# Log-sum rows of the dense units: four small products of a block-diagonal tile, copied to the queries by ScalarE or VectorE in turn

## The chip, the core and the metric

The kernel runs on one core of a Trainium2 chip. The time is that of the device for one execution, in microseconds (us); the median of three runs is compared. The engines, by the profile's names: PE (TensorE, the matmuls; PEld is its loading of weights), DVE (VectorE), ACT (ScalarE), POOL (GpSimd) and SP (SyncE, which issues DMAs here). They run side by side, each in the order of its own instructions, and wait for each other through semaphores. A matmul writes to PSUM; ScalarE and VectorE read it from there.

## The reference

Two attention layers over 2048 positions of 1024 features, with 32 heads of 32 each, and their outputs side by side. Layer B is a sliding window of 256 keys, layer A a dilated window of 8 keys.

```python
def _B_ref(x, wqkv, wo):
    B, S, D = x.shape
    H = 32; Dh = D // H; W = 256
    qkv = (lambda x, *d: x.transpose(*d))((x @ wqkv).reshape(B, S, 3, H, Dh), 2, 0, 3, 1, 4)
    q, k, v = qkv[0], qkv[1], qkv[2]
    scores = jnp.einsum("bhqd,bhkd->bhqk", q, k) * (Dh ** -0.5)
    idx = jnp.arange(S)
    mask = (idx[:, None] - idx[None, :] >= 0) & (idx[:, None] - idx[None, :] < W)
    scores = jnp.where(mask[None, None], scores, -1e9)
    p = _softmax(scores, axis=-1)
    o = jnp.einsum("bhqk,bhkd->bhqd", p, v)
    return (lambda x, *d: x.transpose(*d))(o, 0, 2, 1, 3).reshape(B, S, D) @ wo
```

`_A_ref` has the same projections; each query sees the 8 keys at distances 0, 2, ... 14.

## The kernel before

The work is cut into 8 units of 512 rows: four of layer B (dense) and then four of layer A (windowed). A unit has 8 groups of 4 heads, so there are 32 dense groups. All projections (q and k at L518, v at L583, the output at L645) split each operand into a high and a low part and add three products; the splits are made by `Stream.parts` (L201, L204, L207) from weights that POOL's queue loads (L159).

A dense group is done in two passes. The first (`first`, L857) computes the scores of 128 queries by up to 384 keys, takes the row maximum on VectorE (L862, into `nm`) and the exponential with its row sum on ScalarE (L867, into `sm`): 16 blocks, one for each of 4 query blocks b and 4 heads j. When all 16 are through, `log_sum` takes the logarithm of the sums (L880) and forms `nl` = -(maximum + log-sum), 128 queries by 16, with a high and a low part in `hl` (L885 to L888). `rows` brings these 32 columns into 32 rows of a PSUM tile by one product with the identity (L896), and `spread` writes them to the lower 32 partitions of the stacked queries `q[96:P, j, :]`, once for each head, times a 0/1 tile `pick` which keeps of each row only the block and head that it belongs to (L902). The keys hold ones in these partitions. So the second pass (`second`, L940), which computes the scores again with keys as rows, subtracts maximum and log-sum in the product itself, and its exponential (L947) is the finished probability. Masks are applied by POOL (L926) or VectorE (L929), and `values` multiplies with v (L987).

PSUM is held by rings: 3 tiles for projections, 4 for the scores of both passes and the log-sum rows, 1 for the output of a group.

The order of all instructions is made when the kernel is built. `Clock` books the assumed time of every instruction on its engine. The loop at L1060 takes, from four lists (the log-sum products, the second pass, the first pass, the projections), the item that can start first; an item names its due time by what it waits for, for the second pass `h["rows"]` of its heads and a free PSUM tile (L970). Work of the other engines is issued when the clock reaches it. Waits themselves are put in from what each instruction reads and writes, and hold whether or not the clock foresaw them.

`constants` builds the identity, the masks and `pick` on POOL at the start, ahead of the first loads that POOL issues.

Of the kernel before, what the change touches and what calls it, by code (L numbers as in the profile page):

```python
# [7 lines left out]
F32 = mybir.dt.float32  # L8
# [6 lines left out]
P = 128  # L15
# [21 lines left out]
CW = 1.36  # L37
ORDER = (0, 1, 2, 3, 4, 5, 6, 7)
BANK_LATE = 0.0
EARLY, WARM = 1.0, 10  # L40
TERMS = ((0, 0), (0, 1), (1, 0))

# [174 lines left out]
def kernel(ctx, tc, xs, wqk, wv, wo, outs, units):  # L217
# [87 lines left out]
    def constants():  # L305
        def bands(name, n, keep, fill, *conds):
            m = const.tile([P, n], F32, name=name) if isinstance(name, str) else name
            nc.gpsimd.memset(m, keep)
            for step, base, chan in conds:
                nc.gpsimd.affine_select(m, m, pattern=[[step, n]], compare_op=ALU.is_ge, fill=fill, base=base,  # L310
                                        channel_multiplier=chan)
            return m

        ident = cst["ident"] = const.tile([P, P], F32R, name="ident")
        keep = const.tile([P, P], F32, name="keep_d")
        nc.gpsimd.memset(keep, 0.0)
        nc.gpsimd.affine_select(ident, keep, pattern=[[-1, P]], compare_op=ALU.not_equal, fill=1.0, base=0,
                                channel_multiplier=1)
        pick = cst["pick"] = pickp.tile([32, 16], F32, name="pick")
        nc.gpsimd.memset(pick, 0.0)  # L320
        for row in (0, 16):
            nc.gpsimd.affine_select(pick, pick, pattern=[[-1, 16]], compare_op=ALU.not_equal, fill=1.0, base=-row,
                                    channel_multiplier=1)
        cst["mask_d"] = bands("mask_d", 384, 0.0, FAR, (1, -1, -1), (-1, 256, 1))
        near = cst["near"] = band0[:, :200].rearrange("p (v c) -> p v c", v=5)
        nc.gpsimd.memset(near, 0.0)
        for i in range(4):
            part = near[32 * i:32 * i + 32]
            for step, base, chan in ((1, -1, -1), (-1, 8, 1)):
                nc.gpsimd.affine_select(part, part, pattern=[[0, 5], [step, 40]], compare_op=ALU.is_ge, fill=FAR,  # L330
                                        base=base, channel_multiplier=chan)
        nc.gpsimd.affine_select(near[0:32, 0, :], near[0:32, 0, :], pattern=[[1, 40]], compare_op=ALU.is_ge, fill=FAR,
                                base=-8, channel_multiplier=0)
        cst["keep_f"] = bands("keep_f", P, BIG, 0.0, (-1, -1, 1))
        cst["keep_d"] = bands(keep, P, BIG, 0.0, (1, 0, -1))
        ck.use("pool", 3.0, ck.now)

        def ones():
            zero = cst["mask_d"][96:P, None, P:2 * P].to_broadcast([32, 24, P])
            for t in kst:  # L340
                nc.scalar.activation(t[96:P, :, :].rearrange("p j (a s) -> p (j a) s", s=P), zero, AF.Identity,
                                     bias=1.0, scale=1.0)
                ck.use("act", 2.7, ck.now)

        ck.defer(24.0, ones)

    pfree = [0.0]
    vbuf = [const.tile([P, 6, n * P], F32, name=f"vbuf{i}") for i, (_, n) in enumerate(VPARTS)]
    vpart = {s0 + i: (p, i * P) for p, (s0, n) in enumerate(VPARTS) for i in range(n)}
    tails = const.tile([P, NG, 8], F32, name="tails")  # L350
# [41 lines left out]
    def latest(*ts):  # L392
        return None if any(t is None for t in ts) else max(ts)
# [440 lines left out]
    def attention(u, s):  # L834
# [43 lines left out]
        def log_sum():  # L878
# [4 lines left out]
            def parts():  # L883
                nl = small.tile([P, 16], F32, tag="nl", name="nl")
                nc.vector.tensor_tensor(nl, h["nm"], ln, op=ALU.subtract)  # L885
                hl = small.tile([P, 2, 16], F32R, tag="hl", name="hl")
                nc.vector.tensor_copy(hl[:, 0, :], nl)
                nc.vector.tensor_tensor(hl[:, 1, :], nl, hl[:, 0, :].bitcast(F32), op=ALU.subtract)  # L888
                e2 = ck.use("dve", 0.52, e, port=True)
                aux.append(Item(lambda: latest(rs.when(BANK_LATE), e2), lambda: rows(hl), 0.08))  # L890

            ck.defer(e, parts)

        def rows(hl):
            ps, bank = rs.take()
            nc.tensor.matmul(ps[0:32, 0:P], hl.rearrange("p a b -> p (a b)"), cst["ident"], start=True, stop=True)  # L896

            def spread():

                h["rows"] = []  # L900
                for j in range(4):
                    nc.vector.tensor_tensor(q[96:P, j, :].rearrange("p (b s) -> p b s", s=P),  # L902
                                            ps[0:32, None, 0:P].to_broadcast([32, 4, P]),
                                            cst["pick"][0:32, 4 * j:4 * j + 4, None].to_broadcast([32, 4, P]), op=ALU.mult)
                    e = ck.use("dve", 0.61, ck.now)
                    h["rows"].append(e + ROWS_LATE)
                rs.give(bank, e)

            return spread

# [220 lines left out]
```

## Time and profile before

| What | us |
|---|---|
| runs, median (lowest to highest) | 1831.32 (1831.26 to 1832.84) |
| the profiled execution: its span | 1830.6 |
| TensorE busy | 1807.8 |
| VectorE busy | 1202.9 |
| ScalarE busy | 889.4 |
| POOL busy | 394.4 |

The profiled execution is one of its own; its span is the time from its first to its last instruction. A row of the groups names the line, the engine, the operation, what is written and read with shapes, and the count; behind the bar stand the busy time of all of them, the mean duration of one in ns, and the engine's idle time before them with what ended it. A row of the timeline begins with the start and the duration in us. A row of the waits gives who waited for whom: us in total, how often, the longest. Busy time of TensorE counts each matmul from its start to its modelled end, and these overlap; what one costs is the distance between starts.

### The profile page before, as it was taken

To read this page: it belongs to the slowest core of one execution; us is meant where nothing else is said; L and a number is where in the kernel's file an instruction comes from. 1 tells how busy PE (TensorE), PEld (TensorE's weight loads), DVE (VectorE), ACT (ScalarE), POOL (GpSimd) and SP (SyncE) were. 2 spreads that over 40 slices of the span, in tenths; PEclk is the share of its full clock that TensorE was granted. 3 is DMA by queue.
4 is the path that set the end of the run, shared out by engine and by line. 5 is a ranking of instruction groups with operands and counts; after the bars stand their busy time and mean duration, and the time that the engine had idled before them with its cause. 6 is when DMAs were issued, how large, how long until landed. Compare 5 with 4: busy or idle time off the path is not lost.

```text
span 1830.6 us, 38331 instructions
## 1 busy us (share of the span) xinstructions
PE 1807.8 (99%) x14826; PEld 1477.5 (81%) x14826; DVE 1202.9 (66%) x2694; ACT 889.4 (49%) x2254; POOL 394.4 (22%) x926
## 2 busy tenths in 40 slices
PE   9999999999999999999999999999999999999998
PEld 7787777888778888788887788888888788888887
DVE  6677886768867669777777564655547445655463
ACT  5556466565655655656555343433425234423331
POOL 3322323233242324332233200110001000100000
PEclk9999999999999999999999999999999999999999
DMA  8455665545656456455554343444334443534432
GB/s 242 121 138 139 176 164 150 170 121 160 164 155 164 136 151 183 125 157 141 141 142 130 110 135 116 152 143 130 119 115 143 133 138 108 162 107 128 127 104 83
DMA packets 109141, 257.43 MB, mean 141 GB/s; under 512 B 14496, under 2 KB 29856, under 8 KB 108960
## 3 DMA queue, kind: packets, MB, share of 16 engines
q0 software_dynamic: 41760, 152.06, 28.1%
q1 hardware_dynamic: 56832, 83.00, 17.6%
q10 hardware_dynamic: 10368, 19.93, 3.0%
q8 instruction: 117, 1.92, 0.5%
q14 instruction: 64, 0.52, 0.1%
HBM read 164.63 MB, written 23.07 MB: 103 GB/s over the span
## 4 chain that ended last, share of the span: by engine, by line
PE 92%; DVE 4%; DMA 2%; ACT 2%; issue 1%; SPq 0%; ACTq 0%; POOL 0%; DVEq 0%; POOLq 0%
PE g L518 37%; PE g L645 19%; PE g L583 17%; PE s L940 5%; PE s L857 5%; PE o L987 5%; PE s L711 2%; PE o L774 2%; DMA raw<-xs 1%; DVE w L207 1%; DVE s L862 1%; ACT s L867 0%; DMA qst<-nat 0%; DMA pbuf<-nat 0%; DVE x L207 0%
## 5 line engine op out<-in xcount | busy, mean ns | idle before, releaser
L518 PE MATMUL g<-x,w 128*128 128x512 f32 x3072 | 770.2, 394 | 3.8 <-DVE nm L729 2.4
L518 PEld LDWEIGHTS g<-x,w 128*128 128x128 f32 x3072 | 566.3, 189 | 114.2 <-issue 8.3
L583 PE MATMUL g<-w,x 128*128 128x256 f32 (+1 forms) x2304 | 391.9, 320 | 0.9 <-issue 0.7
L207 DVE TENSOR_TENSOR w<-raw,w 128x512 fp32r<-128x512 f32 x516 | 338.6, 698 | 52.0 <-ACT w L201 44.8
L583 PEld LDWEIGHTS g<-w,x 128*128 128x128 f32 x2304 | 332.3, 190 | 29.2 <-DVE w L207 1.8
L645 PE MATMUL g<-ot,w 128*128 128x512 f32 x1416 | 343.6, 393 | 3.7 <-DVE ot L826 1.8
L867 ACT ACTIVATE s<-s,nm 128x384 f32<-128x384 f32 (+2 forms) x512 | 274.3, 536 | 102.1 <-DVE nm L862 101.8
L862 DVE CUSTOM_DVE_ANT_0 s<-s,mask_d 128x384 f32<-128x384 f32 (+2 forms) x512 | 261.5, 553 | 88.2 <-PE s L857 87.5
L645 PEld LDWEIGHTS g<-ot,w 128*128 128x128 f32 x1416 | 262.4, 188 | 59.3 <-DVE ot L826 3.2
L926 POOL TENSOR_SCALAR_AFFINE_SELECT pbuf<-pbuf 128x128 f32<-128x128 f32 (+1 forms) x606 | 219.8, 391 | 325.1 <-ACT pbuf L947 323.8
L947 ACT ACTIVATE pbuf<-s 128x384 f32<-128x384 f32 (+2 forms) x480 | 202.7, 505 | 72.2 <-PE s L940 70.2
L159 POOL DMA_DIRECT2D raw<-wqk x126 | 68.1, 540 | 457.5 <-DVE w L207 356.3
L204 DVE CAST w<-raw 128x1024 fp32r<-128x1024 f32 x205 | 141.7, 691 | 24.8 <-PE g L518 24.0
L940 PEld LDWEIGHTS s<-qst,kst 128*128 128x128 f32 x704 | 113.0, 188 | 41.2 <-ACT s L867 16.3
L857 PE MATMUL s<-kst,qst 96*128 96x384 f32 (+2 forms) x512 | 142.4, 342 | 0.9 <-ACT s L867 0.6
L940 PE MATMUL s<-qst,kst 128*128 128x256 f32 (+2 forms) x704 | 136.5, 302 | 3.5 <-ACT s L867 3.0
L719 DVE TENSOR_TENSOR band<-s,near 128x160 f32<-128x160 f32 x128 | 32.4, 315 | 158.0 <-PE s L711 158.0
L536 ACT COPY ost<-g 128x512 f32<-128x512 f32 x54 | 31.7, 587 | 207.1 <-PE g L645 200.4
L857 PEld LDWEIGHTS s<-kst,qst 96*128 96x128 f32 x512 | 93.4, 189 | 26.2 <-issue 4.7
L826 DVE TENSOR_TENSOR ot<-o,ot 128x512 fp32r<-128x512 f32 x64 | 44.0, 688 | 101.6 <-ACT ot L822 101.4
L867 ACT ACTIVATION_READ_ACCUMULATOR s<-s,nm 128x1 f32 x512 | 105.3, 206 | 0.0
L159 POOL DMA_DIRECT2D raw<-wo x64 | 34.2, 534 | 304.2 <-DVE w L207 260.2
(77 smaller groups left out, 1298.6 us busy)
## 6 DMA issues: line engine op xcount, KB each, us to landing
raw<-wqk POOLq DMA_DIRECT2D x126, 512.0 KB, 4.3
raw<-wv POOLq DMA_DIRECT2D x72, 512.0 KB, 5.1
raw<-wo POOLq DMA_DIRECT2D x64, 512.0 KB, 4.1
qst<-nat SPq DMA_DIRECT2D x96, 256.0 KB, 5.3
kst<-nat SPq DMA_DIRECT2D x96, 256.0 KB, 5.6
raw<-xs POOLq DMA_DIRECT2D x28, 512.0 KB, 4.6
outs<-ost ACTq DMA_DIRECT2D x56, 256.0 KB, 2.3
kst<-halo SPq DMA_DIRECT2D x72, 128.0 KB, 4.5
```

Source lines behind the costliest of these rows:

```text
L159: (self.nc.scalar if early else self.nc.gpsimd).dma_start(raw if len(ap.shape) == 2 else raw.rearrange("p (a b) -> p a b", a=2), ap)
L204: nc.vector.tensor_copy(t[:, 0, :], raw)
L207: nc.vector.tensor_tensor(t[:, 1, c:c + 512], raw[:, c:c + 512], t[:, 0, c:c + 512].bitcast(F32), op=ALU.subtract)
L518: nc.tensor.matmul(h["ps"], h["w"][:, a, k * P:(k + 1) * P], xt[u][k][:, b, :], start=(k == 0 and i == 0), stop=(k == NK - 1 and i == 2))
L583: nc.tensor.matmul(ps, xt[u][kw * g + k][:, a, p0:p0 + P], h["w"][g][:, c, k], start=(first and t == 0 and half == 0), stop=(last and t == 2),
L645: nc.tensor.matmul(h["ps"], w[:, a, c:c + P], ot[u, k][:, b, :], start=(k == 0 and i == 0), stop=(k == NK - 1 and i == 2))
L857: nc.tensor.matmul(ps[:, :n], q[0:96, j, b * P:(b + 1) * P], kk[0:96, j, c0:c1], start=True, stop=True)
L862: nc.vector.tensor_tensor_reduce(ps[:, :n], ps[:, :n], mask[:, cut:full], scale=-1.0, scalar=BIG, op0=ALU.add, op1=ALU.min, accum_out=nm)
L867: nc.scalar.activation(ps[:, :n], ps[:, :n], AF.Exp, bias=nm, scale=-1.0, accum_out=sm)
L926: nc.gpsimd.affine_select(w, w, pattern=[[0, m], [step, n]], compare_op=ALU.is_ge, fill=0.0, base=base, channel_multiplier=chan)
L940: nc.tensor.matmul(ps[:, i * n:(i + 1) * n], kk[:, j, 256 + kb * P:256 + (kb + 1) * P], q[:, j, q0:q0 + n], start=True, stop=True)
L947: nc.scalar.activation(w, ps[:, :pack * n].rearrange("p (j n) -> p j n", j=pack), AF.Exp)
```

## The change

The 32 columns of `hl` are laid into a tile `turn` of 132 columns, in four blocks of 32 whose starts are 32 apart: block b holds only the values of query block b, at columns 4j + b (high) and 16 + 4j + b (low), and zeros elsewhere. `turn` is cleared once at the start; each group writes the same places again. Four products with the identity, one for each b, fill 32 rows by 512 columns of one PSUM tile. `pick` shrinks to 4 columns: a row is kept for head j or not. Each of the four copies to `q[96:P, j, :]` is then a product with one number per row, and may be done by ScalarE or VectorE; the planner takes the engine that its clock says ends first (0.62 for ScalarE, 0.61 for VectorE), and books them side by side. The booked cost of the products goes from 0.08 to 0.3. `pick` is built by 32 selects of one column in place of 2 of 16.

```diff
-        pick = cst["pick"] = pickp.tile([32, 16], F32, name="pick")
+        pick = cst["pick"] = pickp.tile([32, 4], F32, name="pick")
         nc.gpsimd.memset(pick, 0.0)
-        for row in (0, 16):
-            nc.gpsimd.affine_select(pick, pick, pattern=[[-1, 16]], compare_op=ALU.not_equal, fill=1.0, base=-row,
-                                    channel_multiplier=1)
+        for row in range(0, 32, 4):
+            for b in range(4):
+                c = row // 4 % 4
+                nc.gpsimd.affine_select(pick[:, c:c + 1], pick[:, c:c + 1], pattern=[[0, 1]], compare_op=ALU.not_equal,
+                                        fill=1.0, base=-row - b, channel_multiplier=1)
+        nc.gpsimd.memset(turn, 0.0)
...
+    turn = const.tile([P, 132], F32, name="turn")
...
-                hl = small.tile([P, 2, 16], F32R, tag="hl", name="hl")
-                nc.vector.tensor_copy(hl[:, 0, :], nl)
-                nc.vector.tensor_tensor(hl[:, 1, :], nl, hl[:, 0, :].bitcast(F32), op=ALU.subtract)
+                hl = turn[:, :132].rearrange("p (b x) -> p b x", x=33)
+                hi, lo = [hl[:, :, 16 * a:16 * a + 16:4].bitcast(F32R) for a in range(2)]
+                by = nl.rearrange("p (j b) -> p b j", b=4)
+                nc.vector.tensor_copy(hi, by)
+                nc.vector.tensor_tensor(lo, by, hi.bitcast(F32), op=ALU.subtract)
                 e2 = ck.use("dve", 0.52, e, port=True)
-                aux.append(Item(lambda: latest(rs.when(BANK_LATE), e2), lambda: rows(hl), 0.08))
+                aux.append(Item(lambda: latest(rs.when(BANK_LATE), e2), rows, 0.3))
...
-        def rows(hl):
+        def rows():
             ps, bank = rs.take()
-            nc.tensor.matmul(ps[0:32, 0:P], hl.rearrange("p a b -> p (a b)"), cst["ident"], start=True, stop=True)
+            for b in range(4):
+                nc.tensor.matmul(ps[0:32, b * P:b * P + P], turn[:, 32 * b:32 * b + 32].bitcast(F32R), cst["ident"],
+                                 start=True, stop=True)
...
                 for j in range(4):
-                    nc.vector.tensor_tensor(q[96:P, j, :].rearrange("p (b s) -> p b s", s=P),
-                                            ps[0:32, None, 0:P].to_broadcast([32, 4, P]),
-                                            cst["pick"][0:32, 4 * j:4 * j + 4, None].to_broadcast([32, 4, P]), op=ALU.mult)
-                    e = ck.use("dve", 0.61, ck.now)
-                    h["rows"].append(e + ROWS_LATE)
-                rs.give(bank, e)
+                    if ck.ends("act", 0.62, ck.now) <= ck.ends("dve", 0.61, ck.now) + SPREAD:
+                        nc.scalar.activation(q[96:P, j, :], ps[0:32, :], AF.Copy, scale=cst["pick"][:, j:j + 1])
+                        ends.append(ck.use("act", 0.62, ck.now))
+                    else:
+                        nc.vector.tensor_scalar(q[96:P, j, :], ps[0:32, :], cst["pick"][:, j:j + 1], None, op0=ALU.mult)
+                        ends.append(ck.use("dve", 0.61, ck.now))
+                    h["rows"].append(max(ends) + ROWS_LATE)
+                rs.give(bank, max(ends))
```

`SPREAD` is 0. Since the planner orders everything anew, other instructions move too. In the built program the counts change like this:

| Engine | Before | After |
|---|---|---|
| TensorE, products for the log-sum rows | 32 | 128 |
| VectorE, copies to the queries | 128 | 62 |
| ScalarE, copies to the queries | 0 | 66 |
| VectorE / ScalarE, evacuations of v (L539 / L536) | 10 / 54 | 17 / 47 |
| VectorE / POOL, mask instructions (L929 / L926) | 130 / 606 | 132 / 604 |
| POOL, selects for `pick` | 2 | 32 |

The order around one dense group of the changed program (the 13th, as an example), with the engines that an instruction waits for:

```
TensorE  small product of turn, ident      [VectorE, ScalarE]   x4
TensorE  v projection, 256 columns                              x18
TensorE  second pass, heads 0 to 3         [VectorE, ScalarE] [ScalarE] [VectorE] [ScalarE]
VectorE  copy to the queries, head 0       [TensorE]
ScalarE  copy to the queries, head 1       [VectorE]
VectorE  copy to the queries, head 2       [ScalarE]
ScalarE  copy to the queries, head 3       [VectorE]
```

More of the change, by code (lines that the diff above doesn't have):

```diff
@@ L39 @@
 BANK_LATE = 0.0
+SPREAD = 0.0
 EARLY, WARM = 1.0, 10
@@ L898, in spread @@
             def spread():
                 h["rows"] = []
+                ends = []
                 for j in range(4):
-                    nc.vector.tensor_tensor(q[96:P, j, :].rearrange("p (b s) -> p b s", s=P),
-                                            ps[0:32, None, 0:P].to_broadcast([32, 4, P]),
-                                            cst["pick"][0:32, 4 * j:4 * j + 4, None].to_broadcast([32, 4, P]), op=ALU.mult)
-                    e = ck.use("dve", 0.61, ck.now)
-                    h["rows"].append(e + ROWS_LATE)
```

## The prediction

> **What bounds the kernel now.** I read the page first: busy shares, the strips of 40 slices, the chain of waits.
>
> ```profile
> PE 1807.8 (99%) x14826; PEld 1477.5 (81%) x14826; DVE 1202.9 (66%) x2694; ACT 889.4 (49%) x2254; POOL 394.4 (22%) x926
> ...
> PE   9999999999999999999999999999999999999998
> ...
> DVE  6677886768867669777777564655547445655463
> ACT  5556466565655655656555343433425234423331
> ...
> PE 92%; DVE 4%; DMA 2%; ACT 2%; issue 1%; SPq 0%; ACTq 0%; POOL 0%; DVEq 0%; POOLq 0%
> ```
>
> TensorE is busy in every slice and holds 92% of the chain. VectorE has slack even in the dense units (the first 22 slices, digits 5 to 8). So another matmul costs its full time, and VectorE time saved is worth only what TensorE waits for today. Next I asked for busy time by stretch, and for the waits of TensorE and of its weight loads, in the dense units alone (31 to 1020 us):
>
> ```profile
> 31.00:1020.00 989.00, 980.30 (x5959) 792.38 (x5958) 744.47 (x1927) 576.97 (x1681) 299.60 (x741) 1.00 0.55 150
> ...
> PE s L896 <- DVE hl L888: 3.6, 4, 2.0
> PE s L940 <- ACT s L867: 3.0, 4, 1.1
> ...
> PEld s L940 <- ACT s L867: 16.3, 27, 1.6
> ...
> PEld s L857 <- ACT s L867: 3.7, 15, 0.9
> ```
>
> TensorE (the first busy figure) idles 989.0 - 980.3 = 8.7 us there, 3.6 us of it at L896 for VectorE's log-sum parts. No row of these waits names the copies of L902: all of them are hidden. The third view, groups by line, holds the replaced copies and their nearest relatives (after the bar: busy us, mean ns of one, then idle time before them):
>
> ```profile
> L902 DVE TENSOR_TENSOR qst<-s,pick 32x512 fp32r<-32x512 f32 x128 | 79.3, 676 | 9.9 <-PE s L896 9.4
> ...
> L459 DVE SCALAR_TENSOR_TENSOR nat<-g,nat 128x512 fp32r<-128x512 f32 x64 | 44.0, 688 | 43.5 <-ACT nat L455 43.4
> L455 ACT ACTIVATE nat<-g 128x512 fp32r<-128x512 f32 x64 | 38.3, 598 | 95.2 <-PE g L518 88.6 <-DMA qst<-nat 6.1 <-ACT s L867 0.5
> L536 ACT COPY ost<-g 128x512 f32<-128x512 f32 x54 | 31.7, 587 | 207.1 <-PE g L645 200.4 <-PE s L940 5.5 <-DMA kst<-nat 1.2
> L947 ACT ACTIVATE pbuf<-s 128x384 f32<-128x384 f32 (+2 forms) x480 | 202.7, 505 | 72.2 <-PE s L940 70.2 <-POOL pbuf L926 0.6
> ```
>
> **The change part by part. First the matmuls.** One product of 128 columns becomes four in each of the 32 dense groups: 96 more. Two places of the timeline show the price:
>
> ```profile
> 395.00 0.22 PE L896 MATMUL s<-ident,hl 128*32 128x128 f32 x1
> ...
> 395.06 0.74 PE L857 MATMUL s<-kst,qst 96*128 96x384 f32 x3
> 395.26 2.48 DVE L902 TENSOR_TENSOR qst<-s,pick 32x512 fp32r<-32x512 f32 x4 [0.22 <-PE s L896]
> ...
> 178.15 0.18 DVE L888 TENSOR_TENSOR hl<-nl,hl 128x16 fp32r<-128x16 f32 x1
> ...
> 178.47 0.22 PE L896 MATMUL s<-ident,hl 128*32 128x128 f32 x1 [1.99 <-DVE hl L888]
> ...
> 178.53 1.65 PE L583 MATMUL g<-w,x 128*128 128x256 f32 x12
> ...
> 180.01 0.34 PE L940 MATMUL s<-qst,kst 128*128 128x384 f32 x1
> ```
>
> The next product starts 0.06 us after L896 both times, so the row's 0.22 us is mostly pipeline. 96 x 0.06 = 5.8 us, all on the path. If each had instead to wait out its own 32-column weight load (0.11 us in the row below) it were 10.6 us; below 0.06 I see no reason to go.
>
> ```profile
> 394.89 0.11 PEld L896 LDWEIGHTS s<-ident,hl 128*32 128x32 f32 x1
> ```
>
> **The copies.** Four VectorE copies per group become 66 on ScalarE and 62 on VectorE over the kernel. VectorE's new form (one PSUM operand, a scale per partition) has no row; it lies between L902 at 0.676 and L459 at 0.688 us, so 0.68. ScalarE's is nearest L455, 0.60; L536's 0.587 is the other end. If each engine ran its two alone, the rows would be complete after two copies. The built program says otherwise: in the usual group VectorE's first copy waits for TensorE, ScalarE's first for VectorE's first, VectorE's second for ScalarE's first, ScalarE's second for VectorE's second. All four read one PSUM tile, and the chain is strict. The planner books the two engines side by side (0.62 and 0.61) and places the score products L940 for that. So the stall to price is TensorE arriving before the fourth copy. The price of a hand-over, from two pairs of rows:
>
> ```profile
> 36.88 0.14 DVE L862 DVE_READ_ACCUMULATOR2_ANT nm<- 128x1 f32 x1
> ...
> 37.06 0.45 ACT L867 ACTIVATE s<-s,nm 128x256 f32<-128x256 f32 x1 [1.64 <-DVE nm L862]
> ...
> 19.09 0.60 ACT L455 ACTIVATE nat<-g 128x512 fp32r<-128x512 f32 x1 [4.93 <-PE g L518]
> ...
> 19.72 0.69 DVE L459 SCALAR_TENSOR_TENSOR nat<-g,nat 128x512 fp32r<-128x512 f32 x1 [4.46 <-ACT nat L455]
> ```
>
> VectorE to ScalarE 37.06 - 37.02 = 0.04, back 0.03; VectorE to TensorE 178.47 - 178.33 = 0.14. Counted from the start of the last small product: first copy from 0.26 (395.26 - 395.00) to 0.94; second 0.98 to 1.58; third 1.61 to 2.29; fourth 2.33 to 2.93; TensorE may go at 3.07. Before, the fourth ended at 0.26 + 2.48 = 2.74, on one engine. The hand-overs eat the whole gain.
>
> When does TensorE come? In 12 of the 32 groups the built program has nine 512-column products (or eighteen of 256) behind the small ones, then L940 for heads 0 to 3 in a row. A 256-column product takes (180.01 - 178.53) / 12 = 0.123; a 512-column one 10.88 / 48 = 0.227:
>
> ```profile
> 1101.60 10.88 PE g L645 x48
> ```
>
> Head 3 is then due at 0.06 + 9 x 0.227 + 3 x 0.06 = 2.28 (nine groups) or 2.45 (three), and stalls 0.79 or 0.62 us: 9 x 0.79 + 3 x 0.62 = 9.0 us. In these groups nothing stands on VectorE between the parts and the first copy, so it does start at 0.26. Nine more groups come by the same sum to 0.45 twice and 0.44 (head 3 due at 2.6), 0.1 three times (due at 2.96), about 1 twice (a weight split stands before VectorE's copies) and 1.6 once (head 0 due at 0.3): together 5.2 us. The other 11 have enough products in between. Stalls: 14.2 us. Both ends: 0, if TensorE comes later than the built order says; 14.2 + 21 x 0.4 = 22.6 us if each of the four hand-overs takes 0.1 more.
>
> **What queues behind the waiting copies.** ScalarE is held from its first wait to 2.93. In eight groups an evacuation of 512 columns (0.59) stands next, and only then the first exponential of L940's results, which must free a PSUM bank: 2.93 + 0.59 + 0.45 (256 columns, as at 37.06 above) = 3.97. TensorE, having gone on at 3.07 with four 256-column products, wants the bank at 3.6: 0.35 x 8 = 2.8 us, between 0 and double. VectorE is free at 2.29 instead of 2.74; what waits there, mainly weight splits, gains nothing that TensorE waits for.
>
> [...]
>
> **The start.** 32 selects of one column replace two of 16, ahead of the first weight loads on POOL:
>
> ```profile
> 1.49 0.45 POOL L322 TENSOR_SCALAR_AFFINE_SELECT pick<-pick 32x16 f32<-32x16 f32 x2
> ...
> 10.02 1.19 POOL L159 DMA_DIRECT2D raw<-wqk  x2 [0.30 <-issue]
> ...
> 20.32 0.68 DVE L204 CAST w<-raw 128x1024 fp32r<-128x1024 f32 x1
> ...
> 22.43 5.44 ACT L341 ACTIVATE kst<-mask_d 32x3072 fp32r<-32x3072 f32 x2
> ...
> raw<-wqk POOLq DMA_DIRECT2D x126, 512.0 KB, 4.3
> ```
>
> 30 x 0.2 plus a memset of 0.2 move the load from 10.0 to 16.2; landing after 4.3 it is there at 20.5, where the cast now starts at 20.32: 0.2 us, and between 0 and 2. The masks behind the selects come 6 us later too, all issued by 16 us; the first reader in this view, L341, starts at 22.43. The four-column pick and the strided parts (16 elements each, like L888's) I cost at nothing.
>
> **Sum.** 5.8 + 14.2 + 2.8 + 0.2 = 23.0 us on the profiled span of 1830.6; the median of the runs is 0.7 above it. Forecast 1854.3, rounded to 1854, 1.2% slower. Its own range takes half to one and a half of the two waits (17.0 us) and the matmuls at 5.8 to 10.6: 1845 to 1867.
>
> **Rivals.** A: the copies' chain is hidden, because TensorE itself runs behind the planner's clock, as the copies of L902 were. Then 5.8 to 6.6 us: 1838. For it: today nothing waits for L902. Against: today L940 comes where the planner put it for four serial copies.
> B, the other side: VectorE's relief. 66 x 0.68 = 45 us less work in the dense units lets the row maxima come earlier, the exponentials too, and so the PSUM banks that L940 and L857 wait for. Price: at most those weight-load waits, 16.3 + 3.7 = 20.0 us, and what is left of the 8.7 us of idle. It decides from 5.8 us on, if the chain of copies costs nothing; half of the 20 gives 5.8 - 10 = -4.2: 1827. Against it: 744 of 989 us busy, and a VectorE held at each ScalarE copy.
> C: ScalarE's holding spreads: in every group the later PSUM banks come two exponentials of L947 late, 2 x 0.505 us; 32 x 1.0 + 14.2 + 5.8 = 52 us: 1883. Against: ScalarE is 58% busy there (577 of 989) and catches up in a few us.
>
> **How the numbers follow.** Forecast 0.72, A 0.13, B 0.08, C 0.07. The range 1838 to 1868 adds A to the forecast's own and leaves out B and C. A measurement of this kernel can tell 0.2% (3.7 us) from no change. Faster: most of B, 0.06; within: the rest of B and A's edge, 0.06; slower 0.88.
>
> **What would show it.** Small products 0.06 us apart and 128 of them; copies alternating on the two engines without overlap, the fourth ending near 2.9; TensorE waiting before L940 for ScalarE's copies, some 14 us in all, where L902 had none; the first weight load issued near 16 us. Copies that overlap, or no such waits, would make me wrong.

## The result and the profile after

| | before | changed |
|---|---|---|
| median of the runs, us | 1831.29 (4 runs) | 1882.97 (1880.78 to 1885.20, 4 runs) |
| ratio | 1 | 1.0282, 95% interval 1.0267 to 1.0296 |
| span of the profiled execution, us | 1830.6 | 1880.8 |

The change costs 51.6 us, 29 more than the forecast and 15 above the end of its range. (Where effects are given in us below, they are differences of ratios times 1831.3, since each group of runs had its own runs of the kernel before. A range in brackets behind an effect goes by the intervals of the ratios.) The page of the changed kernel, in the lines that answer to those of before: busy times, and the chain of waits by engine and by line.

```profile
PE 1846.0 (98%) x14922; PEld 1494.8 (79%) x14922; DVE 1168.5 (62%) x2633; ACT 935.1 (50%) x2317; POOL 409.5 (22%) x955
...
PE 88%; DVE 4%; ACT 3%; DMA 2%; issue 1%; POOL 1%; POOLq 0%; ACTq 0%; DVEq 0%; SPq 0%
PE g L523 36%; PE g L650 18%; PE g L588 16%; PE s L952 5%; PE s L862 4%; PE o L999 4%; PE s L716 2%; PE o L779 2%; DVE qst L916 2%; DMA raw<-xs 1%; ACT qst L913 1%; DVE x L208 1%; DVE w L208 1%; DVE s L867 1%; ACT s L872 0%
```

The lines of the chain before:

```profile
PE g L518 37%; PE g L645 19%; PE g L583 17%; PE s L940 5%; PE s L857 5%; PE o L987 5%; PE s L711 2%; PE o L774 2%; DMA raw<-xs 1%; DVE w L207 1%; DVE s L862 1%; ACT s L867 0%; DMA qst<-nat 0%; DMA pbuf<-nat 0%; DVE x L207 0%
```

Two things meet the eye. The copies (L916 on VectorE, L913 on ScalarE) stand in the chain with 2% and 1%, 51 us of steps, where L902 is not listed. And TensorE is busy 38 us longer although 96 short products are all that was added to it: a matmul that takes longer is busy, too, so something has slowed matmuls that did not change. The stretch of the dense units (31 us to shortly before the first windowed unit), the waits of TensorE and VectorE, and the copies among the groups by line. A row of a stretch gives its bounds and length, then the busy time and count of TensorE, its weight loads, VectorE, ScalarE and POOL, and last the granted clock, the DMA share and GB/s:

```profile
31.00:1072.00 1041.00, 1019.87 (x6122) 813.43 (x6121) 712.00 (x1869) 623.83 (x1751) 312.29 (x753) 0.99 0.51 144
```

```profile
PE s L952 <- ACT qst L913: 7.1, 19, 0.8
PE s L862 <- ACT s L872: 5.1, 6, 1.2
PE s L952 <- DVE qst L916: 3.8, 7, 1.5
...
DVE x L205 <- DMA raw<-xs: 21.3, 4, 6.9
```

```profile
L916 DVE TENSOR_SCALAR qst<-s,pick 32x512 fp32r<-32x512 f32 x62 | 45.8, 743 | 43.1 <-ACT qst L913 25.0 <-PE s L904 17.9
L913 ACT ACTIVATE qst<-s,pick 32x512 fp32r<-32x512 f32 x66 | 43.6, 675 | 91.0 <-DVE qst L916 81.2 <-PE s L904 9.5
```

TensorE now waits 7.1 + 3.8 = 10.9 us for the copies before the second pass, and 5.1 us for exponentials of the first pass. Each engine waits for the other's copy: 25.0 us on VectorE, 81.2 us on ScalarE. The copies take 0.743 and 0.675 us where 0.61 and 0.62 are booked. One group in the timeline, TensorE's rows, then VectorE's, then ScalarE's:

```profile
407.89 0.40 PE L904 MATMUL s<-ident,turn 128*32 128x128 f32 x4
408.13 2.36 PE L588 MATMUL g<-w,x 128*128 128x256 f32 x18
410.32 0.61 PE L952 MATMUL s<-qst,kst 128*128 128x128 f32 x3
411.32 1.03 PE L952 MATMUL s<-qst,kst 128*128 128x128 f32 x6 [0.38 <-ACT qst L913]
...
408.33 0.74 DVE L916 TENSOR_SCALAR qst<-s,pick 32x512 fp32r<-32x512 f32 x1 [0.99 <-PE s L904]
409.82 0.74 DVE L916 TENSOR_SCALAR qst<-s,pick 32x512 fp32r<-32x512 f32 x1 [0.74 <-ACT qst L913]
...
409.11 0.68 ACT L913 ACTIVATE qst<-s,pick 32x512 fp32r<-32x512 f32 x1 [2.55 <-DVE qst L916]
410.59 0.68 ACT L913 ACTIVATE qst<-s,pick 32x512 fp32r<-32x512 f32 x1 [0.81 <-DVE qst L916]
```

Four products in 0.24 us, then the chain, engine by engine: 408.33, 409.11, 409.82, 410.59. The last copy ends at 411.27, and head 3's score product, in place behind 18 products of 256 columns, starts at 411.32. This is the prediction's picture. Head 3 was due 3 x 0.06 us behind 410.32, at 410.50, and so stalls 0.82 us. What the prediction has no term for is in TensorE's granted clock. In eight stretches the trace shows it at half speed (0.50); five of them:

```profile
24.50:27.90 3.40, 3.03 (x7) 2.42 (x8) 3.33 (x6) 3.40 (x2) 1.06 (x1) 0.50 1.03 295
184.90:191.70 6.80, 6.56 (x30) 5.17 (x23) 4.52 (x8) 4.70 (x10) 3.20 (x9) 0.50 0.97 208
...
481.90:485.20 3.30, 3.30 (x9) 2.56 (x8) 3.23 (x13) 2.17 (x7) 0.69 (x1) 0.50 0.53 138
748.10:751.50 3.40, 3.28 (x9) 2.69 (x9) 3.33 (x14) 1.98 (x8) 0.70 (x1) 0.50 0.42 101
1014.40:1017.70 3.30, 3.23 (x8) 2.49 (x8) 3.23 (x13) 2.26 (x10) 0.71 (x1) 0.50 0.34 62
```

All eight, 34 us at half speed, cost some 17, if their work would else have taken half the time; before, the only such stretch ahead of the very end is 3.4 us at 10.7. The last three shown (482, 748, 1014) stand 266 us apart: the boundaries between dense units. What happens there, from POOL's, VectorE's, ScalarE's and TensorE's timelines:

```profile
454.19 6.71 POOL L938 TENSOR_SCALAR_AFFINE_SELECT pbuf<-pbuf 128x128 f32<-128x128 f32 x12 [4.09 <-ACT pbuf L959]
460.85 1.58 POOL L160 DMA_DIRECT2D raw<-xs  x3
...
468.53 0.43 DVE L205 CAST x<-raw 128x512 fp32r<-128x512 f32 x1 [6.89 <-DMA raw<-xs]
...
473.44 0.56 ACT L872 ACTIVATE s<-s,nm 128x384 f32<-128x384 f32 x1 [3.29 <-DVE nm L867]
...
474.16 2.13 PE L862 MATMUL s<-kst,qst 96*128 96x384 f32 x4 [0.50 <-ACT s L872]
476.13 2.27 PE L523 MATMUL g<-x,w 128*128 128x512 f32 x6
479.65 2.13 PE L862 MATMUL s<-kst,qst 96*128 96x384 f32 x4 [1.25 <-ACT s L872]
```

Three loads of the next unit's x are issued behind 12 masks. VectorE stands 6.9 us at the split of x; the row maxima that stand behind it come late, with them the exponentials, and TensorE waits. At 481.9 its clock falls. Before, VectorE's waits for x came to 2.9 us in the whole run:

```profile
DVE x L204 <- DMA raw<-xs: 2.9, 3, 1.6
```

### The profile page after: what moved, and what is told of

It is laid out like the page before. It is cut to its first block, busy times and chain, and to the rows that moved or that the text cites. A ratio compares the mean times of both kernels' runs of the same rounds, so it can differ in the third digit from the quotient of the medians.

```text
span 1880.8 us, 38557 instructions
## 1 busy us (share of the span) xinstructions
PE 1846.0 (98%) x14922; PEld 1494.8 (79%) x14922; DVE 1168.5 (62%) x2633; ACT 935.1 (50%) x2317; POOL 409.5 (22%) x955
## 4 chain that ended last, share of the span: by engine, by line
PE 88%; DVE 4%; ACT 3%; DMA 2%; issue 1%; POOL 1%; POOLq 0%; ACTq 0%; DVEq 0%; SPq 0%
PE g L523 36%; PE g L650 18%; PE g L588 16%; PE s L952 5%; PE s L862 4%; PE o L999 4%; PE s L716 2%; PE o L779 2%; DVE qst L916 2%; DMA raw<-xs 1%; ACT qst L913 1%; DVE x L208 1%; DVE w L208 1%; DVE s L867 1%; ACT s L872 0%
## 5 line engine op out<-in xcount | busy, mean ns | idle before, releaser
L523 PE MATMUL g<-x,w 128*128 128x512 f32 x3072 | 775.2, 397 | 5.5 <-DVE w L205 2.6
L523 PEld LDWEIGHTS g<-x,w 128*128 128x128 f32 x3072 | 573.9, 190 | 120.3 <-issue 4.8
L588 PE MATMUL g<-w,x 128*128 128x256 f32 (+1 forms) x2304 | 394.3, 321 | 1.2 <-issue 1.0
L588 PEld LDWEIGHTS g<-w,x 128*128 128x128 f32 x2304 | 334.8, 191 | 28.6 <-issue 2.7
L650 PE MATMUL g<-ot,w 128*128 128x512 f32 x1416 | 352.8, 397 | 1.1 <-DVE ot L831 1.1
L650 PEld LDWEIGHTS g<-ot,w 128*128 128x128 f32 x1416 | 262.6, 188 | 58.9 <-DVE ot L831 1.6
L938 POOL TENSOR_SCALAR_AFFINE_SELECT pbuf<-pbuf 128x128 f32<-128x128 f32 (+1 forms) x604 | 226.8, 407 | 287.8 <-ACT pbuf L959 285.5
L952 PEld LDWEIGHTS s<-qst,kst 128*128 128x128 f32 x704 | 112.8, 192 | 57.3 <-ACT s L872 17.0
L952 PE MATMUL s<-qst,kst 128*128 128x256 f32 (+2 forms) x704 | 145.0, 313 | 11.8 <-ACT qst L913 7.1
L862 PE MATMUL s<-kst,qst 96*128 96x384 f32 (+2 forms) x512 | 149.5, 346 | 6.7 <-ACT s L872 5.1
L160 POOL DMA_DIRECT2D raw<-wv x72 | 46.3, 643 | 272.9 <-DVE w L208 187.0
```

What stands on the lines that cost most here:

```text
L160: (self.nc.scalar if early else self.nc.gpsimd).dma_start(raw if len(ap.shape) == 2 else raw.rearrange("p (a b) -> p a b", a=2), ap)
L523: nc.tensor.matmul(h["ps"], h["w"][:, a, k * P:(k + 1) * P], xt[u][k][:, b, :], start=(k == 0 and i == 0), stop=(k == NK - 1 and i == 2))
L588: nc.tensor.matmul(ps, xt[u][kw * g + k][:, a, p0:p0 + P], h["w"][g][:, c, k], start=(first and t == 0 and half == 0), stop=(last and t == 2),
L650: nc.tensor.matmul(h["ps"], w[:, a, c:c + P], ot[u, k][:, b, :], start=(k == 0 and i == 0), stop=(k == NK - 1 and i == 2))
L862: nc.tensor.matmul(ps[:, :n], q[0:96, j, b * P:(b + 1) * P], kk[0:96, j, c0:c1], start=True, stop=True)
L938: nc.gpsimd.affine_select(w, w, pattern=[[0, m], [step, n]], compare_op=ALU.is_ge, fill=0.0, base=base, channel_multiplier=chan)
```

## The experiments

Two theories to begin with. W: the copies' hand-overs are the loss. L: the plan is the loss, as the figures booked for products and copies are not what runs, and the whole order has shifted with them.

**The parts alone.** Kernel before, its product issued four times at the old booking; then the changed kernel with 8 selects for `pick`; with all copies on VectorE; with each copy booked behind the one ahead of it.

```diff
-            nc.tensor.matmul(ps[0:32, 0:P], hl..., cst["ident"], start=True, stop=True)
+            for b in range(4):
+                nc.tensor.matmul(ps[0:32, b * P:b * P + P], hl..., cst["ident"], start=True, stop=True)
```

> The kernel before, with its log-sum product issued four times into four column blocks of the PSUM tile, the same booking, copies and select tile as before; the order of all other instructions is the same. Theory P (the 96 products cost 0.06 us each, nothing else moves): 1831.3 + 5.8 = 1837, copies of L902 still hidden. Rival Q (the products come out worse, by their weight loads or by pushing the second pass late): 1842 or more.

1833.02 us, ratio 1.0009 (0.9999 to 1.0018): 1.7 us, 3.3 at most. The four products cost less than the 5.8 us that the forecast has for them.

```diff
-        for row in range(0, 32, 4):
+        for row in range(0, 32, 16):
             for b in range(4):
-                nc.gpsimd.affine_select(pick[:, c:c + 1], pick[:, c:c + 1], pattern=[[0, 1]], ...
+                nc.gpsimd.affine_select(pick, pick, pattern=[[-4, 4]], ...
```

> The changed kernel, its four-column select tile built by 8 selects over all columns in place of 32 over one; every other engine's order is the same. Theory S (the selects delay the first loads by 24 x 0.3 = 7 us, which costs about 3 us of waiting and 1.7 us of half clock at the start, and nothing later): 1883 - 4.5 = 1878.5, the wait for the first late weight gone. Rival T (the start is made up for later, or was a late transfer by chance): within 1 us of 1883.

1880.74 us, 1.0260 (1.0243 to 1.0278): 4 us less by the ratios, 2.2 by the medians, intervals overlapping. With the second such pair, further down, the start is worth 0 to 4 us.

```diff
-SPREAD = 0.0
+SPREAD = -100.0
```

> The changed kernel, all four copies on VectorE (no chain over two engines, and the planner books them one after the other as they run). Theory W (the loss is the chain of copies that the planner books side by side, with the half clock and late loads that follow from it): products 5.8 + start 4.5 remain, 1842, no wait of the second pass for copies. Rival L (the loss is the load: products and copies of 0.74 us, whoever does them): 1870 or more. Rival X (the planner's new order of masks and loads on POOL does it): three waits of the first pass of 0.7 to 1.4 us at the unit boundaries remain, 1855 to 1865.

1877.45 us, 1.0243 (1.0226 to 1.0260). With no hand-over between engines left, only 7 us less. Theory W as the whole is out, though this also shifts the order.

```diff
-                ends = []
+                ends = [ck.now]
...
-                    if ck.ends("act", 0.62, ck.now) <= ck.ends("dve", 0.61, ck.now) + SPREAD:
+                    if ck.ends("act", 0.68, ends[-1]) <= ck.ends("dve", 0.74, ends[-1]) + SPREAD:
```

(and the two bookings likewise)

> The changed kernel, with the same alternation allowed, but each copy booked to start when the one before ends, at the measured 0.74 and 0.68 us. The planner then gives most copies to ScalarE. Theory W: TensorE arrives after the copies, so no wait for them; products 5.8 + start 4.5: 1842, up to 1850 for ScalarE's longer hold. Rival L: 1870 or more.

1848.63 us, 1.0089 (1.0074 to 1.0104). Two thirds of the loss are gone. But two things changed at once: the order, and the engine, since by honest figures the planner gives 123 of the 128 copies to ScalarE.

**Order and copies apart.** Kernel before with 0.3 booked for its product (later 0.14); the changed copies, all on VectorE, with all bookings as before, so that the rest is ordered as before; the same with copies 1 and 3 forced to ScalarE; and the serial booking with 8 selects.

```diff
-                aux.append(Item(lambda: latest(rs.when(BANK_LATE), e2), lambda: rows(hl), 0.08))
+                aux.append(Item(lambda: latest(rs.when(BANK_LATE), e2), lambda: rows(hl), 0.3))
```

First with 0.3:

> The kernel before, in which only the figure that the plan books for the product is raised from 0.08 to 0.3 us, as the change has it; every instruction of the log-sum rows is as before. The order that is written out shifts with it: 21 masks move from VectorE to GpSimd. Theory P (the loss is the reshuffled order: masks on GpSimd ahead of the loads of x at the unit boundaries): 1865 to 1880 us, with x loads that land near 468 us. Theory R (the loss is the real copies, 0.74 and 0.68 us in a chain, which the plan books as 0.61 side by side): within 4 us of the kernel before, about 1833 us.

1858.27 us, 1.0134 (1.0111 to 1.0156): between the two. Nothing that is executed differs from the kernel before but which engine does 22 masks and one evacuation, and where things stand, and 25 us are lost. At the first boundary the four loads of x are issued at 436.7 to 446.8 us here, 428.4 to 442.7 before and 449.0 to 461.9 in the changed kernel, and VectorE's waits for x come to 7.5 us; TensorE's waits show late exponentials, 8.3 us, against 0.6 for this pair before:

```profile
PE s L857 <- ACT s L867: 8.3, 9, 1.2
PE s L896 <- DVE hl L888: 7.2, 4, 2.9
```

This pair before:

```profile
PE s L857 <- ACT s L867: 0.6, 1, 0.6
```

The same line with 0.14:

> The kernel before with the product booked at 0.14 instead of 0.08 us, the smallest shift of the plan: 14 masks move to GpSimd, nothing that is executed for the log-sum rows changes. If the loss of the plan-only kernel (25 us at 0.30) is due to the size of the false booking, this one loses a quarter of it or less: 1833 to 1840 us. If any other order than the one that the kernel before had costs as much: 1845 to 1860 us.

1836.96 us, 1.0030 (1.0020 to 1.0041). A small shift costs 5.5 us: the loss of an order is no fixed tax of leaving the tuned one, it depends on which order comes out.

```diff
-SPREAD = 0.0
+SPREAD = -100.0
...
-                aux.append(Item(lambda: latest(rs.when(BANK_LATE), e2), rows, 0.3))
+                aux.append(Item(lambda: latest(rs.when(BANK_LATE), e2), rows, 0.08))
```

> All four copies on VectorE, and the product booked at 0.08 us: what is booked is then what the kernel before books, so the order of the rest is that of the kernel before, with the small products and the real copies (0.66 to 0.74 us) in it. Theory P (order): about 1840 us, that is before plus some 2 us for the products, 2 to 5 for the start and little else. Theory R (real copies longer than booked): 1865 us or more, as with the all-VectorE kernel under the changed plan (1877).

1849.81 us, 1.0085 (1.0062 to 1.0109), 10 more than theory P has. In its trace the first group comes 10.1 us late, with this wait near the start; what the other 6 us were shows only below.

```profile
PE s L862 <- DMA kst<-nat: 4.9, 1, 4.9
```

```diff
-                    if ck.ends("act", 0.62, ck.now) <= ck.ends("dve", 0.61, ck.now) + SPREAD:
+                    if j % 2 == 1:
                         nc.scalar.activation(...)
-                        ends.append(ck.use("act", 0.62, ck.now))
                     else:
                         nc.vector.tensor_scalar(...)
-                        ends.append(ck.use("dve", 0.61, ck.now))
+                    ends.append(ck.use("dve", 0.61, ck.now))
```

(and 0.08 for the product)

> Copies 0 and 2 on VectorE and 1 and 3 on ScalarE, always, but booked as four copies of 0.61 us on VectorE, so that the order of the rest is that of the kernel before. Theory P (order): 1838 to 1850 us, even though the copies are handed from engine to engine as in the changed kernel. Theory R: 1865 us or more. Theory W (the hand-overs alone, 16 us of TensorE's waits before the score products): 1855 us.

1879.78 us, 1.0255 (1.0236 to 1.0274): neither. Here ScalarE's copies are in no booking, and TensorE pays for that in the first pass, behind ScalarE:

```profile
PE s L862 <- ACT qst L913: 12.4, 5, 3.2
PE s L951 <- ACT qst L913: 6.1, 6, 1.3
```

The serial booking and the 8 selects, both as above:

> The changed kernel with each copy booked after the end of the copy ahead of it, at 0.74 and 0.68 us, and with the block-diagonal scale tile made by 8 selects instead of 32. Next to the kernel with the serial booking alone (1848.6): every theory expects 2 to 3 us less, 1846 us, since the first loads of GpSimd start earlier. If the start costs as much as its profile shows (the first group 4.8 us later), 1844 us.

1850.05 us, 1.0091 (1.0072 to 1.0110): no gain from 8 selects here.

**The hand-over and the loads of x, in the changed kernel's own order.** ScalarE's copies read a constant of SBUF, so that the log-sum rows that it should write are left out; x comes by SyncE's queue; both. In these kernels TensorE, VectorE and ScalarE run the very sequence of the changed kernel.

```diff
-                        nc.scalar.activation(q[96:P, j, :], ps[0:32, :], AF.Copy, scale=...)
+                        nc.scalar.activation(q[96:P, j, :]..., cst["ident"]...[0:32, None, :].to_broadcast([32, 4, P]), AF.Copy, scale=...)
```

> The changed kernel with its own order, in which ScalarE's copies read a constant tile of SBUF instead of the product in PSUM, so that neither engine waits for the other (the queries' log-sum rows that ScalarE writes are then wrong values; nothing is left out of the work). Theory H (the copies of one product, handed from engine to engine, cost about 16 us of TensorE's waits directly and as much again in late exponentials and clock): 1845 to 1862 us. Theory B (the late loads of x at the unit boundaries): 1870 us or more. The two trade places in the next kernel.

1865.42 us, 1.0179 (1.0156 to 1.0203): the hand-overs cost 18.9 us (14 to 24), a little over a third of the loss. The direct waits before L952 are gone but for 2.6 us; half speed stays at 34 us. ScalarE's copies take 0.713 us there, not less than the 0.675 of the changed kernel, so the gain is not that of shorter copies.

```diff
-            (self.nc.scalar if early else self.nc.gpsimd).dma_start(raw if ...
+            (self.nc.scalar if early else self.nc.sync if self.items[self.loaded][0] == "x" and self.loaded > 16 else self.nc.gpsimd).dma_start(raw if ...
```

> The changed kernel with its own order, in which the 28 loads of x of units 1 to 7 are issued on SyncE's queue instead of GpSimd's, so that no mask stands ahead of them; all else is unchanged. Theory B (the late loads of x cost about 10 us at each of three boundaries, with the stalls and the clock behind them): 1850 to 1860 us, x landing within 10 us of its issue in the order and VectorE's waits for x (21 us) below 8 us. Theory H (the hand-over): 1875 us or more.

1882.29 us, 1.0271 (1.0248 to 1.0293): no gain, but the edit did not do what it was for. SyncE has its own work ahead of the three loads, and VectorE waits for x nearly as long as in the changed kernel (17.4 against 21.3 us):

```profile
457.86 1.88 SPq L484 DMA_DIRECT2D qst<-nat  x3
459.83 1.86 SPq L484 DMA_DIRECT2D kst<-nat  x3
461.73 0.61 SPq L474 DMA_DIRECT2D halo<-nat  x1
462.52 1.54 SPq L160 DMA_DIRECT2D raw<-xs  x3
...
DVE x L205 <- DMA raw<-xs: 17.4, 3, 6.9
```

So this run says nothing on what late x costs.

Both edits together:

> Both edits together: ScalarE's copies read a constant, and x is loaded from SyncE's queue. If the two causes are separate and add: before plus the start (5 us), the products (2 us) and what is left, 1838 to 1848 us. If they are one cause seen twice: the same as the better of the two alone.

1860.53 us, 1.0156 (1.0135 to 1.0176), 4 us below the run without hand-overs, with intervals that overlap: far from 1838 to 1848. Some 29 us had still no name.

**The place of the tiles.** Sorted by line, TensorE's distances between starts showed one that had grown where nothing had been touched, that of the output projection L650, and in every kernel so far that has the tile `turn`: 0.233 us in the median, 0.227 before. A run of 48 of these products in the timeline of the kernel before, and one in that of the changed kernel:

```profile
1101.44 11.04 PE L645 MATMUL g<-ot,w 128*128 128x512 f32 x48
```

```profile
1127.55 11.36 PE L650 MATMUL g<-ot,w 128*128 128x512 f32 x48
```

`turn` (528 bytes a partition) and the smaller `pick` have moved all tiles behind them. In the built programs the weights `w`, v and x begin at a multiple of 64 bytes before, and 32 bytes past one after; `ot` begins at a multiple of 64 in both.

```diff
-        pick = cst["pick"] = pickp.tile([32, 4], F32, name="pick")
+        pick = cst["pick"] = pickp.tile([32, 16], F32, name="pick")[:, :4]
...
-    turn = const.tile([P, 132], F32, name="turn")
+    turn = const.tile([P, 144], F32, name="turn")
```

> The changed kernel with its own order; only two tiles are padded (turn from 528 to 576 bytes a partition, pick to 64), so that every tile behind them begins at a multiple of 64 bytes again, as in the kernel before. Theory A (the place of the tiles sets the pace of the output projection's 1536 products, 233 ns against 227): their pace falls back to 227 ns and the time to 1872 to 1876 us. Theory N (the pace has another cause, such as the order around them): 233 ns and 1881 to 1884 us as the changed kernel.

1872.08 us, 1.0227 (1.0205 to 1.0249): 10.1 us (5 to 15) for two paddings. The row of L650 is back, and its median distance is 0.227 us again; 1536 products x 0.006 us are 9.2 us:

```profile
1124.07 11.04 PE L650 MATMUL g<-ot,w 128*128 128x512 f32 x48
```

These paddings with the serial booking and the 8 selects:

> The changed kernel with the copies booked one after the other at what they take (0.74 and 0.68 us), 8 selects instead of 32, and the two tiles padded. Without the padding it took 1850.1. Theory A: about 8 us less, 1840 to 1844 us, that is within 0.7% of the kernel before. Theory N: 1848 to 1852 us. No theory has it faster than the kernel before, whose copies cost TensorE nothing that could be saved.

1835.95 us, 1.0030 (1.0019 to 1.0040), 11 us under the unpadded one, and 5.5 us slower than before. By its waits and the rows by line, x is in time, ScalarE does the copies, and TensorE does not wait for them:

```profile
DVE x L205 <- DMA raw<-xs: 0.6, 1, 0.6
...
L912 ACT ACTIVATE qst<-s,pick 32x512 fp32r<-32x512 f32 x123 | 73.5, 666 | 44.0 <-PE s L903 43.2 <-DVE qst L915 0.6
```

The all-VectorE kernel with an honest figure:

```diff
-SPREAD = 0.0
+SPREAD = -100.0
...
-                        ends.append(ck.use("dve", 0.61, ck.now))
+                        ends.append(ck.use("dve", 0.74, ck.now))
```

> All four copies on VectorE, booked at 0.74 us each, which is what most of them take, instead of 0.61 us; the product is booked at 0.30 us as in the change. With the false booking it took 1877.5 us. Theory M (a plan that books less than what runs puts work in VectorE's queue ahead of what TensorE needs): 1845 to 1855 us. Theory V (VectorE's load of 70 us more, or the order as such): 1870 us or more.

1868.60 us, 1.0207 (1.0186 to 1.0228): 7 us less than with 0.61, where theory M wants 22 or more. An honest booking by itself does not mend the order; the serial kernel had nearly all copies on ScalarE as well. Nor is late x needed for such a loss, as VectorE's waits for it are short here:

```profile
DVE x L205 <- DMA raw<-xs: 6.8, 6, 3.8
```

The all-VectorE kernel in the old order once more, with the 8 selects and the two paddings:

> All four copies on VectorE with the order of the kernel before, 8 selects and the two tiles padded. Without selects and padding mended it took 1849.8 us. If the log-sum rows themselves cost nothing under the old order, the start (10 us late at the first group there) and the pace (8 us) were all of it: 1832 to 1838 us. If the longer copies cost TensorE time: 1840 us or more.

1834.81 us, 1.0018 (1.0003 to 1.0033). Under the old order the new products and copies cost 3.3 us (0.5 to 6). So in the unpadded kernel of this order the other 12 us were start and place together.

**What is left.** The constant source of ScalarE's copies, the 8 selects and the paddings in one kernel, all as above:

> The changed kernel with its own order, in which ScalarE's copies read a constant (the rows that ScalarE writes are wrong values; no work is left out), with 8 selects and the two tiles padded. If the parts add (10 for the place, 17 for the hand-over, 2 for the start off 1882.5): 1851 to 1855 us, and the 20 us that stay above the kernel before are the order's and the longer copies'. If the parts overlap, as the clock would make them: 1838 to 1846 us.

1849.95 us, 1.0097 (1.0080 to 1.0113). 17.8 us (15 to 21) are left, about what adding gives (51.6 less 10.1, 18.9 and 0 to 4: 18.6 to 22.6). Three of its six stretches at half speed, and two rows of its waits:

```profile
176.40:183.20 6.80, 6.57 (x30) 5.17 (x23) 4.49 (x8) 4.74 (x10) 3.33 (x10) 0.50 0.90 204
...
466.60:470.00 3.40, 3.40 (x9) 2.63 (x8) 3.33 (x13) 2.21 (x7) 0.72 (x1) 0.50 0.52 145
726.00:732.80 6.80, 6.78 (x16) 5.00 (x17) 6.66 (x20) 5.13 (x17) 0.71 (x1) 0.50 0.48 150
```

```profile
PE s L861 <- ACT s L871: 4.8, 6, 1.2
...
DVE x L205 <- DMA raw<-xs: 20.2, 4, 6.6
```

In all 27.2 us at half speed cost some 13.6, reckoned as above, 12 more than before's 3.4 us do; the late exponentials add some 4 directly. VectorE's waits for x are still there.

And the changed kernel with 8 selects and paddings, hand-overs and all, with the old figure for the product:

```diff
-                aux.append(Item(lambda: latest(rs.when(BANK_LATE), e2), rows, 0.3))
+                aux.append(Item(lambda: latest(rs.when(BANK_LATE), e2), rows, 0.08))
```

> The changed kernel, with 8 selects and the two tiles padded, and the product booked at 0.08 us as before instead of 0.30; the copies are booked and handed over as in the change. With 0.30 the time would be about 1870 (1872.1 less 2 for the start). If the 0.30 is what spoils the order, as it cost 25 us in the kernel before: 1845 to 1855 us. If the copies booked side by side spoil it: 1866 to 1872 us.

1870.93 us, 1.0205 (1.0187 to 1.0223), about as with 0.30 and paddings (1872.08, there with 32 selects; the intervals overlap). The 0.30 that cost the kernel before 25 us is not what spoils the changed kernel's order; there it was a false figure, here the four products do take 0.24 us. No kernel tried beats the kernel before.

## Why the prediction was wrong

In us, by the ratios:

| Part | Forecast | Measured | By |
|---|---|---|---|
| small products | 5.8 | 1.7, at most 3.3 | the kernel before with four products |
| chain of copies and ScalarE's hold | 14.2 + 2.8 | 18.9 (14 to 24) | the changed order without hand-overs |
| start | 0.2 | 0 to 4 | 8 selects, in two pairs of kernels |
| place of the tiles | none | 10.1 (5 to 15) | the padded kernel |
| order of the rest, with the clock that falls in it | none | 17.8 (15 to 21) with the products and longer copies in it | what is left without the three above |

The first terms, 23.0 forecast, come to 21 to 26 measured, by the middle of the intervals. **The step that failed is the sum:** it set four terms on the span of the old kernel as if the rest ran on unchanged, so it put the new order of the rest and the place of the tiles at nothing, without a reason. The runs show 17.8 us for the one, the products and longer copies included, and 10.1 us for the other. The prediction's own material had a trace of both: the planner orders everything anew, and a new tile pushes the other tiles on.

**Products.** 0.06 us apart, as read. That 96 x 0.06 is all on the path was too much; where TensorE took back the rest no run shows.

**Copies.** The strict chain is there: no copy overlaps one of the other engine (two in a row on one engine overlap by 0.08 to 0.09 us). In the group above it ends 3.2 us behind the last product's start (411.27 - 408.07), not 2.93, as the copies take 0.74 and 0.68 and not 0.68 and 0.60; a hand-over between the two costs 0.03 to 0.04, as taken from the rows, the last one, to TensorE, 0.05 and not 0.14. So head 3 stalls 0.82 us there, where the forecast for such a group has 0.62. The rows of the waits, 10.9 us, count only from the modelled end of the product before; from start to start, outside the stretches at half speed, the stalls that a copy ended come to some 17 us, an estimate from this trace. Stalls and hold together, 17.0 forecast, agree with 18.9 within its interval; how much of that is the hold no run shows. No run here shows what reads of the one tile by both engines side by side would do, as no such kernel was tried.

**Start.** The first weight load is issued at 19.6 us, not 16.2, mainly because a select takes 6.96 / 26 = 0.27 us, not 0.2.

```profile
1.49 6.96 POOL L325 TENSOR_SCALAR_AFFINE_SELECT pick<-pick 32x1 f32<-32x1 f32 x26
...
19.61 1.19 POOL L160 DMA_DIRECT2D raw<-wqk  x2 [0.30 <-issue]
```

**The rivals.** C named 1883, which is what came, but by luck: the run without hand-overs also ends ScalarE's holding, and gives back 18.9 us where C's two waits make 46. A, the hidden chain at 1838, is what the serial booking reaches with the other parts mended (1836). B has no run in its favour: in none did VectorE's freed time make the kernel faster than before. (VectorE's digits in the first 22 slices are 6 to 9, not 5 to 8 as read, so its slack was smaller than stated.)

**The order** is the part with the least certain cause. Shown: 17.8 us stay when hand-overs, start and place are gone. Of these, 12 go by the sum above to TensorE at half speed. Seen in the traces, not isolated: late x, late maxima, late exponentials, then the low clock, at each boundary of dense units (in the changed kernel VectorE stands 6.9, 5.5 and 5.0 us for x there, and TensorE each time 1.25 us for an exponential); in the padded serial kernel x is in time (0.6 us of waits) and half speed is down to 6.8 us. Late x is not the only way: the all-VectorE kernel with an honest booking waits 6.8 us for x, has no hand-over between engines, and loses 38 us, some 10 of them by place, as its products of L650 start 0.233 us apart, too. Open: how much of the loss goes away if x alone comes in time, since the attempt left the loads late.

## What to carry to other kernels

Where a planner writes the order out from booked times, a change has two prices, its own work and the new order; measure them apart by running the new work under the old bookings, and the new bookings with the old work. Book what runs: copies that the built program makes wait for each other are booked one after the other; here that gave 123 of the 128 to one engine. After adding a tile, compare the distance between starts of matmuls that were not touched: 6 nanoseconds each, from a new address, were 9 of the 10 us here.

## What the runs showed of the hardware

**The clock.** In the changed kernel TensorE fell to half speed (a granted clock of 0.50) for 3.4 or 6.8 us after stalls shorter than that. Ahead of 481.88 it idles 1.25 us (to 479.65) and pauses three times for 0.4 us; in the 3.41 us to the fall it still does four products of 384 columns and one of 512, about a quarter of the time at 0.227 us for 512 columns. The 3.41 us is taken from the trace: the shortest whole stretch at half speed lasts 3.413 us, and all changes of the granted clock stand multiples of that apart (the falls at 481.88, 748.12 and 1014.37 by 78 each). By the same 0.227 us, with products that overlap counted once, the traces of the kernel before and of the changed one were cut into stretches of 3.41 us, counted from the nearest fall, from 31 us to shortly before the end. In the changed kernel there are six falls, behind stretches in which columns streamed for 19 to 41% of the time; of its other stretches at full speed the emptiest has 47%. In the kernel before none brought a fall, though four had only 32, 36, 41 and 43%. So the share of such a stretch alone does not tell: 32% went without a fall in one kernel, and 41% (ahead of 215.65) brought one in the other. Nor does the length of a stall: 2.0 us of idle ahead of 178.47 in the kernel before brought no fall, and 1.25 us ahead of 479.65 stands before one. What decides was not shown.

**The address.** With `w` 32 bytes past a multiple of 64 and `ot` on one, products of 512 columns start 0.233 us apart (median of L650 in the changed kernel), with both on a multiple 0.227 (before, and in the padded kernel). Products in which both operands had moved by the same 32 bytes (L523, L588) kept their pace: 0.227 us for 512 columns and 0.120 for 256 in both kernels. It was tried for this one pair of places only.
